# TensorE order of attention pairs 4 to 15: four runs of one array mode a pair, score stages between runs, small pieces evicted together

## The chip, the cores and the metric

The kernel runs on one core of a Trainium2 chip. The metric is the device time of one launch in microseconds (us); the kernel before takes 1127.12 us, the median of 3 runs (1125.73 to 1127.14). TensorE (PE) multiplies matrices and transposes, VectorE (DVE), ScalarE (ACT) and GpSimd (POOL) work on elements, and SyncE (SP) issues most transfers.

## The reference

Attention with a bias from a small network, then two feed-forward layers, all in float32.

```python
# attention: B, H, S, D = 4, 8, 576, 64; hidden 32
scores = q @ k^T / sqrt(D)
x      = log1p(|i - j|) / log1p(max(i, 1))          # (S, S, 1)
bias   = relu(x @ w1 + b1) @ w2                     # (S, S, H), the same for every batch
attn   = softmax(scores + bias);  o = attn @ v
x      = o as (2304 tokens, 512)
# layer 1                                # layer 2
h = x @ w_in;  g = h * cos(h)            # h = x @ w_in;  g = max(h,0) + alpha*min(h,0)
x = g @ w_out                            # out = g @ w_out
```

Sizes of the layers: 512 to 2048 and back, 2304 tokens.

## The kernel before

The attention works on 16 **pairs**: two heads of one batch. The 576 queries of a pair are four tiles of 128 (stages 1 to 4, both heads each) and a remainder of 64, taken for both heads together (stage 0). Tiles 0 and 1 are unit A, tiles 2 and 3 with the remainder unit B. Pairs 0 to 3 run all units A first, since their bias is still being computed; from pair 4 (`FIRST`) on, a pair runs A, then B.

A **score stage** (`emit_S`, L448) is six steps on TensorE. For stages 1 to 4 each step is two matmuls over 64 rows of the array, one head each, side by side; stage 0 uses all 128 rows. All stages write one PSUM tile (`ps_s`, `bufs=1`), so that a stage can start when the two DVE operations of the stage before (L464: add bias, scale, take the minimum of the negated scores) have read it. ACT then takes the exponential in place (L477).

What follows a unit is a list of **fillers** (L585), one letter each: `0` to `3` transpose the probabilities of 128 keys (`T_full`, eight or four 128x128 transposes into one PSUM bank of three, then a copy to SBUF by DVE, "v", or ACT, "a"); `R` does this for the remainder (`T_rem`); `L` and `M` transpose the last 64 keys (`T_last`, and `T_corner` for the remainder); `N` and `O` transpose the reciprocal row sums (`norm`, `norm_last`), copied by ACT; `v w x y z` multiply by V, 128 keys each, the first four with two 64-column halves of the array and `z` with all of it; `x_out` multiplies by the reciprocals and stores.

So TensorE changes between three **modes**: 64 rows (`64*128` in the profile: scores), 128x128 (transposes, stage 0, `z`) and 64 columns (`128*64`: products with V, corners).

**What sets the order.** The program emits a stage, then as many fillers as a credit allows (L693 to L698). Around this a list scheduler with a timing model reorders all engines' instructions, except where `keep_in_program_order` pins them; the matmuls of the attention are not pinned. Beside the attention run conversions of the weights (`conv`, `wi`, `stage_wo`), a few steps after each stage. `stage_wo` makes four high/low pairs per step in one staging buffer (`sw`): ACT copies the high part (L242), POOL subtracts (L244), SP stores (L259), and the next may start when the store has landed. Then the first layer starts (`h_phase0`, L757).

Of the kernel before, what the change touches and what calls it, by code (L numbers as in the profile page):

```python
# [9 lines left out]
F32 = mybir.dt.float32  # L10
# [18 lines left out]
HS = S // 2  # L29
# [41 lines left out]
def attn_mlp_kernel(ctx: ExitStack, tc: tile.TileContext, a: dict, out: bass.AP):  # L71
# [259 lines left out]
    def attention():  # L331
        with ExitStack() as c:
# [47 lines left out]
            def t_bank(name):  # L380
                return turn("t", ps_t).tile([128, 512], F32, tag="t", name=name)
# [52 lines left out]
            def emit_S(n, s):  # L434
                q, k = qk[n][::len(qk[n]) // 2]
                terms = ((q, k),)
                if n >= NFP:
                    qh, ql, kh, kl = qk[n]
                    terms = ((qh, kh), (qh, kl), (ql, kh))
                both = ps_s.tile([128, 4, 512], F32, tag="s", name=f"S{n}_{s}")  # L440
                pss = [both[:, 2 * h:2 * h + 2] for h in range(2 if s else 1)]
                for hf in range(2):
                    for j, (w, m) in enumerate(terms):
                        for h, ps in enumerate(pss):
                            r, i = (slice(64 * h, 64 * h + 64), s - 1) if s else (slice(0, 128), 4)
# [46 lines left out]

            def corner(ps, w):
                for h in range(2):
                    te.matmul(ps[64 * h:64 * h + 64, 256:320], lhsT=w, rhs=ident[:, 64 * h:64 * h + 64],
                              start=True, stop=True)

            def norm_last(n, u):
                Nt[n, u] = t_bank(f"N{n}_{u}")
                corner(Nt[n, u], Rt[n, u][:, 4, :])  # L500

            def norm(n, u):
                t, rem = SIZE[u]
                rb = Rt[n, u]
                ps = Nt.pop((n, u)) if rem else t_bank(f"N{n}_{u}")
                for x in range(t):
                    te.transpose(out=ps[:, 128 * x:128 * x + 128],
                                 in_=rb[:, 2 * x:2 * x + 2, :].rearrange("p a b -> p (a b)"), identity=ident)
                R = x_p.tile([128, 320], F32, tag="R", name=f"R{n}_{u}")
                cpy("a", R[:, 0:QW[u]], ps[:, 0:QW[u]])  # L510
                Rt[n, u] = R

            def cpy(eng, o, i):
                if eng == "a":
                    keep(4, se.activation(out=o, in_=i, func=AF.Copy))
                else:
                    keep(5, ve.tensor_copy(out=o, in_=i))

            def T_full(n, u, k, eng):
                t, rem = SIZE[u]  # L520
                if k == 0:
                    Tt[n, u] = T_p.tile([128, 4, 2, 320], F32, tag="T", name=f"T{n}_{u}")
                ps = t_bank(f"T{n}_{u}_{k}")
                m = 2 // t
                for d in range(m):
                    for h in range(2):
                        for x, i in enumerate(UNIT[u][0]):
                            o = 256 * d + 128 * t * h + 128 * x
                            cc = m * k + d
                            te.transpose(out=ps[:, o:o + 128], in_=Pp[n, i][:, (S + 64) * h + 128 * cc:(S + 64) * h + 128 * cc + 128],  # L530
                                         identity=ident)
                with tc.high_priority(offset=CPRI):
                    cpy(eng, Tt[n, u][:, m * k:m * k + m, :, 0:128 * t], ps.rearrange("p (c h q) -> p c h q", c=m, h=2))

            def T_rem(n, u, eng):
# [7 lines left out]
            def T_corner(n, u):
                T5t[n, u] = t_bank(f"T5{n}_{u}")
                corner(T5t[n, u], Pt[n, 0, 0][:, 512:S])

            def T_last(n, u, eng):
                T5 = T_p.tile([128, 320], F32, tag="T5", name=f"T5{n}_{u}")
                ps = T5t.pop((n, u)) if SIZE[u][1] else t_bank(f"T5{n}_{u}")
                T5t[n, u] = T5  # L550
                for x, i in enumerate(UNIT[u][0]):
                    te.transpose(out=ps[:, 128 * x:128 * x + 128], in_=Pp[n, i][:, 512:640], identity=ident)
                cpy(eng, T5[:, 0:QW[u]], ps[:, 0:QW[u]])

            def PV(n, u, cc):
                v = vt[n]
                w = QW[u]
                if cc == 0:
                    xps[n, u] = turn("x", ps_x).tile([128, 512], F32, tag="x", name=f"x{n}_{u}")
                ps = xps[n, u]  # L560
                if cc == 4:
                    te.matmul(ps[:, 0:w], lhsT=v[:, 512:640], rhs=T5t.pop((n, u))[:, 0:w], start=False, stop=True)
                else:
                    for h in range(2):
                        te.matmul(ps[64 * h:64 * h + 64, 0:w],  # L565
                                  lhsT=v[:, 256 * h + 64 * cc:256 * h + 64 * cc + 64],
                                  rhs=Tt[n, u][:, cc, h, 0:w], start=(cc == 0), stop=False)

            def x_out(n, u):
                hp, b = pairs[n]  # L570
                w = QW[u]
                ps = xps.pop((n, u))
                del Tt[n, u]
# [7 lines left out]
                ve.tensor_tensor(out=x[:, 0:w], in0=ps[:, 0:w], in1=Rt.pop((n, u))[:, 0:w], op=ALU.mult)  # L581
                at0 = b * S + 128 * UNIT[u][0][0]
                sy.dma_start(out=x_d[hp, :, at0:at0 + w], in_=x[:, 0:w])

            def fillers(n, u):  # L585
                t, rem = SIZE[u]
                e = TENG[u]
                ops = {str(k): (0.44, lambda k=k: T_full(n, u, k, e[k])) for k in range(2 * t)}
                ops.update({"vwxyz"[k]: (0.00167 * QW[u], lambda k=k: PV(n, u, k)) for k in range(5)})
                ops["L"] = (0.11 * t, lambda: T_last(n, u, e[4]))  # L590
                ops["N"] = (0.11 * t, lambda: norm(n, u))
                ops["M"] = (0.1, lambda: T_corner(n, u))
                ops["O"] = (0.1, lambda: norm_last(n, u))
# [60 lines left out]
            while i < NS or pend_exp or waiting or fill:  # L654
                new = []
                if i < NS:
                    n, u, s = stages[i]
                    hp, b = pairs[n]
                    more_bias(max(BFIRST + int(BRATE * j), GNEED[s]))
                    for m in range(FIRST, NP):  # L660
# [33 lines left out]
                while fill and (credit > 0 or i >= NS):  # L694
                    d, fn = fill.pop(0)
                    credit -= d
                    fn()
                if not fill:  # L698
                    credit = min(credit, 0.0)
# [491 lines left out]
```

## Time and profile before

| | |
|---|---|
| median of the runs | 1127.12 us |
| profiled execution, its span | 1125.42 us, 1123.6 us |
| PE busy | 1078.8 us (96%) |
| DVE, ACT, POOL busy | 823.8 (73%), 639.7 (57%), 251.3 us (22%) |
| granted TensorE clock | 0.993 of full speed on average |
| chain that ended last | PE 78%, DVE 9%, DMA 6%, ACT 3% |

The attention fills about the first 346 us. A busy share of PE says little here: a matmul's recorded duration covers its way through the array, and the next one starts long before it ends. The time of a step is read from start to start. In the timeline, one row merges equal instructions that follow each other; the first number is the start of the first of them.

### The profile page before, as it was taken

The numbers are of one execution on the slowest core, as the hardware profiler recorded it, in microseconds if no ns is written. First come the engines' busy times: TensorE is split into PE (matmuls) and PEld (weight loads), VectorE is DVE, ScalarE is ACT, GpSimd is POOL, SyncE is SP. The second block draws the span as 40 slices with busy tenths as digits, with TensorE's granted clock in tenths as the row PEclk, the third lists the DMA queues.
The fourth block names the chain that finished last, engine by engine and source line by source line (L and its number), as shares of the span: only waits on it lengthen the run. The fifth ranks groups of instructions, "written<-read, shape, count | busy, mean of one in ns | idle before, by whom it ended". The sixth has DMA issues, their size and how long they took to land.

```text
span 1123.6 us, 18901 instructions
## 1 busy us (share of the span) xinstructions
PE 1078.8 (96%) x7078; PEld 895.2 (80%) x7078; DVE 823.8 (73%) x1336; ACT 639.7 (57%) x1068; POOL 251.3 (22%) x248
## 2 busy tenths in 40 slices
PE   7698999999998998999999999999999999999998
PEld 2245666666666877888799999998888889999998
DVE  8886777777775789787877787857766756767673
ACT  6886767777775555455455454446555534444442
POOL 4304655656433121000000000222322210000000
PEclk9889999999999999999999999999999999999999
DMA  8666645656447774543766445596666649664621
GB/s 276 216 172 194 188 153 184 207 186 232 153 144 276 300 253 150 160 141 124 251 225 201 174 142 196 171 345 210 207 228 205 208 146 344 208 204 127 211 66 48
DMA packets 107659, 219.77 MB, mean 196 GB/s; under 512 B 11568, under 2 KB 57392, under 8 KB 106160
## 3 DMA queue, kind: packets, MB, share of 16 engines
q1 hardware_dynamic: 77104, 157.74, 43.9%
q10 hardware_dynamic: 28032, 50.34, 12.0%
q0 software_dynamic: 2432, 10.49, 2.4%
q8 instruction: 56, 0.92, 0.3%
q14 instruction: 35, 0.29, 0.1%
HBM read 133.98 MB, written 84.56 MB: 194 GB/s over the span
## 4 chain that ended last, share of the span: by engine, by line
PE 78%; DVE 9%; DMA 6%; ACT 3%; issue 2%; POOL 1%; SPq 1%; ACTq 0%; DVEq 0%; POOLq 0%
PE v L1086 17%; PE ob L955 14%; PE h L757 11%; PE oc L955 9%; PE oa L955 8%; PE S L448 6%; PE x_B L565 3%; DVE u L134 3%; PE T_A L530 2%; PE x_A L565 2%; PE T_B L530 2%; DMA a<-g_d 1%; DMA w_d<-sw 1%; DVE P L464 1%; PE bps L139 1%
## 5 line engine op out<-in xcount | busy, mean ns | idle before, releaser
L1086 PE MATMUL v<-x,v 128*128 128x512 f32 (+1 forms) x984 | 198.0, 364 | 0.0
L1086 PEld LDWEIGHTS v<-x,v 128*128 128x128 f32 x984 | 168.5, 189 | 29.5
L757 PE MATMUL h<-xhi,w 128*128 128x512 f32 (+1 forms) x640 | 184.7, 372 | 7.4 <-DVE tb L770 7.0
L757 PEld LDWEIGHTS h<-xhi,w 128*128 128x128 f32 x640 | 116.1, 188 | 30.9 <-issue 7.4
L226 POOL TENSOR_TENSOR wc<-wc,wp 128x512 int32<-128x512 int32 x64 | 85.5, 1337 | 214.2 <-DVE wc L223 162.7
L477 ACT ACTIVATE P<-P,nm 128x576 f32<-128x576 f32 x128 | 98.5, 771 | 42.9 <-DVE nm L464 42.4
L757 PE MATMUL h<-xlo,w 128*128 128x512 f32 (+1 forms) x320 | 118.5, 370 | 0.0
L937 ACT ACTIVATE op<-a 128x768 fp32r<-128x768 f32 x84 | 70.6, 845 | 83.3 <-PE ob L955 27.3
L938 DVE TENSOR_TENSOR op<-a,op 128x768 fp32r<-128x768 f32 x84 | 80.0, 957 | 50.8 <-ACT op L937 49.9
L464 DVE CUSTOM_DVE_ANT_0 P<-S,bt 128x576 f32<-128x576 f32 x128 | 91.9, 753 | 32.0 <-PE S L448 24.4
L937 ACT ACTIVATE op<-b 128x768 fp32r<-128x768 f32 x84 | 70.7, 844 | 67.9 <-PE ob L955 22.2
L938 DVE TENSOR_TENSOR op<-b,op 128x768 fp32r<-128x768 f32 x84 | 79.9, 955 | 32.9 <-ACT op L937 32.8
L955 PE MATMUL ob<-op,wo 128*128 128x384 f32 x432 | 76.4, 336 | 0.0
L1097 DVE SCALAR_TENSOR_TENSOR u<-v,asg,u 128x1024 f32<-128x1024 f32 (+2 forms) x48 | 48.0, 1013 | 38.2 <-ACT u L1096 37.9
L955 PEld LDWEIGHTS ob<-op,wo 128*128 128x128 f32 x432 | 75.1, 188 | 0.0
L765 ACT ACTIVATE ta<-h,quart 128x1024 int32<-128x1024 f32 (+1 forms) x40 | 41.1, 1027 | 52.1 <-PE h L757 25.7
L757 PEld LDWEIGHTS h<-xlo,w 128*128 128x128 f32 x320 | 60.3, 189 | 10.8
L448 PE MATMUL S<-kh,qh 64*128 64x288 f32 (+1 forms) x270 | 53.0, 348 | 13.8 <-DVE nm L464 13.7
L1096 ACT ACTIVATE u<-v,sgn 128x1024 f32<-128x1024 f32 (+2 forms) x48 | 43.0, 898 | 38.7 <-PE v L1086 38.7
L766 DVE SCALAR_TENSOR_TENSOR tb<-ta,h 128x1024 f32<-128x1024 int32 (+1 forms) x40 | 44.4, 1110 | 23.5 <-ACT ta L765 22.5
L134 DVE TENSOR_SCALAR u<-at,thr 128x576 f32<-128x576 f32 (+17 forms) x120 | 54.3, 522 | 2.3 <-PE bps L139 2.2
L217 ACT ACTIVATE wp<-raw 128x512 int32<-128x512 uint32 x64 | 42.5, 664 | 21.6 <-POOL wc L226 10.5
(153 smaller groups left out, 2157.9 us busy)
## 6 DMA issues: line engine op xcount, KB each, us to landing
a<-g_d SPq DMA_DIRECT2D x60, 384.0 KB, 4.9
b<-g_d SPq DMA_DIRECT2D x48, 384.0 KB, 5.3
raw<-in_wi_dram SPq DMA_DIRECT2D x32, 512.0 KB, 4.0
raw<-in_wo_dram SPq DMA_DIRECT2D x32, 512.0 KB, 4.3
g_d<-tb ACTq DMA_DIRECT2D x32, 512.0 KB, 3.1
g_d<-u ACTq DMA_DIRECT2D x28, 512.0 KB, 3.3
bias_d<-be SPq DMA_DIRECT2D x36, 295.5 KB, 3.5
w_d<-sw SPq DMA_DIRECT2D x35, 256.0 KB, 2.6
```

What stands on the lines that cost most here:

```text
L134: ve.tensor_scalar(u[:, 0:n], at[:, 0:n], thr[:, m:m + 1], None, op0=ALU.max)
L226: ge.tensor_tensor(out=c, in0=c, in1=p, op=ALU.add)
L448: te.matmul(ps[:, hf, 0:HS], lhsT=w[r, 128 * i:128 * i + 128], rhs=m[r, c0:c0 + HS], start=(j == 0), stop=(j == len(terms) - 1))
L464: keep(2, ve.tensor_tensor_reduce(out=sn.rearrange("p (a b) -> p a b", a=2), in0=ps[:, :, 0:HS], in1=bt[hp, s].rearrange("p (a b) -> p a b ...
L477: keep(3, se.activation(out=e, in_=e, func=AF.Exp, bias=nm, scale=-1.0, accum_out=sums[n, u][:, col, 0:1]))
L565: te.matmul(ps[64 * h:64 * h + 64, 0:w], lhsT=v[:, 256 * h + 64 * cc:256 * h + 64 * cc + 64], rhs=Tt[n, u][:, cc, h, 0:w], start=(cc == 0) ...
L757: te.matmul(ps, lhsT=w_[:, wx, w], rhs=xx[:, 0:n], start=(j == 0), stop=(j == 11))
L937: se.activation(out=o[:, 0], in_=x, func=AF.Copy)
L938: lows.append(ve.tensor_tensor(out=o[:, 1], in0=x, in1=o[:, 0].bitcast(F32), op=ALU.subtract))
L955: ins = te.matmul(ps[:, m], lhsT=x[:, sl] if L else w[:, sl], rhs=w if L else x, start=first, stop=kk == NK - 1 and n == 2, skip_group_che ...
L1086: ins = te.matmul(both[:, i, 0:a1 - a0], lhsT=w[:, wx, 128 * cc:128 * cc + 128], rhs=x[:, xx, cc, a0 - o:a1 - o], start=(n == 0), stop=(n ...
L1097: ve.scalar_tensor_tensor(out=g, in0=ps, scalar=asg[:, f:f + 1], in1=g, op0=ALU.mult, op1=ALU.max)
```

## The change

From pair 4 on (`steady`) every matmul of the attention is pinned, so that TensorE's order is the order of emission. Stages of a pair come as 1, 0, 2, 3, 4. The fillers carry a kind, and each stage lets out fillers of certain kinds until one of another kind heads the list. That gives four runs a pair: after stage 1 and around stage 0 one of 128x128 work, after stage 2 one of 64-column work, after stage 3 one of 128x128 work, after stage 4 one of 64-column work. What unit A leaves (`L`, `N`, `z`, `x_out`) is a tail that is put into B's first run, and the reverse.

`L` and `N` now share one PSUM bank and are copied together by ACT (128x512), and so are `M` and `O` (128x128). DVE copied `L` before. The tile `R` goes; `T5` holds both.

```diff
-TENG = {"A": "vava-a", "B": "vavava"}
+RUNS = {"A": ("01^23", "vwxy"), "B": ("R0^123", "vwxyMO")}
+TENG = {"A": "vavaaaa", "B": "vavaaaa"}
...
+            first = next(i for i, x in enumerate(stages) if x[0] == FIRST)
+            stages[first:] = [(n, u, s) for n in range(FIRST, NP) for u, s in (("A", 1), ("B", 0), ("A", 2), ("B", 3), ("B", 4))]
+            steady = []
+            tails = []
+            def pe(ins):
+                return tc.keep_in_program_order(ins) if steady else ins
...
+            def pieces(n, u):
+                if (n, u) not in T5t:
+                    T5t[n, u] = T_p.tile([128, 2, 320], F32, tag="T5", name=f"T5{n}_{u}")
+                return T5t[n, u]
+            def T_corner(n, u):
+                Nt[n, u] = t_bank(f"C{n}_{u}")
+                corner(Nt[n, u][:, 0:64], Pt[n, 0, 0][:, 512:S])
+            def norm_last(n, u, eng):
+                ps = Nt.pop((n, u))
+                corner(ps[:, 64:128], Rt[n, u][:, 4, :])
+                cpy(eng, pieces(n, u)[:, :, 256:320], ps[:, 0:128].rearrange("p (a q) -> p a q", a=2))
+            def T_last(n, u):
+                Nt[n, u, 0] = t_bank(f"L{n}_{u}")
+                for x, i in enumerate(UNIT[u][0]):
+                    pe(te.transpose(out=Nt[n, u, 0][:, 128 * x:128 * x + 128], in_=Pp[n, i][:, 512:640], identity=ident))
+            def norm(n, u, eng):
+                ps = Nt.pop((n, u, 0))
...
+                cpy(eng, pieces(n, u)[:, :, 0:256], ps.rearrange("p (a q) -> p a q", a=2))
...
-                return [ops[k] for k in ORDER[u]] + [(0.0, lambda: x_out(n, u))]
+                if steady:
+                    head, rest = RUNS[u][0].split("^")
+                    old = tails.pop() if tails else []
+                    if (n, u) == (NP - 1, "B"):
+                        return old[0:2] + [(*ops[k], 1) for k in head] + old[2:] + [(*ops[k], 1) for k in rest + "MOLN" + "vwxyz"] + [(0.0, out, 1)]
+                    tails.append([(*ops["L"], 1), (*ops["N"], 1), (*ops["z"], 1), (0.0, out, 1)])
+                    return (old[0:2] + [(*ops[k], 1) for k in head] + old[2:] + [(*ops[k], 3) for k in rest] +
+                            [(*ops[k], 2) for k in RUNS[u][1]])
+                return [(*ops[k], 0) for k in ORDER[u]] + [(0.0, out, 0)]
...
+                if steady:
+                    if i >= NS and not pend_exp and not waiting:
+                        fill += tails.pop() if tails else []
+                    want = {1: (0, 1), 0: (0, 3), 2: (0, 2), 3: (0, 1, 3), 4: (0, 2)}[s] if i < NS else range(4)
+                    while fill and fill[0][2] in want:
+                        fill.pop(0)[1]()
```

**TensorE between stage 4 of pair 7 and stage 1 of pair 8.** `S` are the scores (`S_4` stage 4), `x_A` products with V, `N_A` reciprocals, `T_B` and `Tr` transposes. Before:

```order
L448 MATMUL S_4_2625<-kh_2269,ql_2267 128x288 x2
L565 MATMUL x_A<-T_A,v_2110 64x256 x4
L507 MATMUL N_A<-ident,rb_A 128x128 x2
L565 MATMUL x_A<-T_A,v_2110 64x256 x2
L530 MATMUL T_B_2854<-ident,P_2_2579 128x128
L565 MATMUL x_A<-T_A,v_2110 64x256 x2
L562 MATMUL x_A<-T_A,v_2110 128x256
L530 MATMUL T_B_2896<-ident,P_2_2579 128x128
L539 MATMUL Tr_2902<-ident,Pr_2528 128x128 x4
L448 MATMUL S_1_2678<-kh_2518,qh_2515 128x288 x2
```

Now, at the same place:

```order
L457 MATMUL S_4_2665<-kh_2274,ql_2272 128x288 x2
L575 MATMUL x_A<-T_A,v_2140 64x256 x8
L457 MATMUL S_1_2707<-kh_2531,qh_2528 128x288 x2
L457 MATMUL S_1_2707<-kl_2532,qh_2528 128x288 x2
L457 MATMUL S_1_2707<-kh_2531,ql_2529 128x288 x2
L457 MATMUL S_1_2707<-kh_2531,qh_2528 128x288 x2
L457 MATMUL S_1_2707<-kl_2532,qh_2528 128x288 x2
L457 MATMUL S_1_2707<-kh_2531,ql_2529 128x288 x2
L524 MATMUL L_A<-ident,P_0_2446 128x128
L524 MATMUL L_A<-ident,P_1_2547 128x128
L529 MATMUL L_A<-ident,rb_A 128x128 x2
L561 MATMUL Tr_2740<-ident,Pr_2500 128x128 x4
```

Six groups of two modes between the stages have become one group; `N_A` and `Tr` moved behind stage 1.

**TensorE where pair 3 ends and pair 4 begins**, now (`S_3` and `S_4` are pair 3's, `S_1` is pair 4's, `x_B` belongs to pair 2):

```order
L457 MATMUL S_3_1553<-kh_527,ql_525 128x288 x2
L575 MATMUL x_B<-T_B,v_678 64x320 x2
L457 MATMUL S_4_1611<-kh_527,qh_524 128x288 x2
L457 MATMUL S_4_1611<-kl_528,qh_524 128x288 x2
L457 MATMUL S_4_1611<-kh_527,ql_525 128x288 x2
L457 MATMUL S_4_1611<-kh_527,qh_524 128x288 x2
L457 MATMUL S_4_1611<-kl_528,qh_524 128x288 x2
L457 MATMUL S_4_1611<-kh_527,ql_525 128x288 x2
L457 MATMUL S_1_1658<-kh_1508,qh_1505 128x288 x2
```

Before, ten rows of fillers stood between `S_3` and `S_4`, and eight between `S_4` and `S_1`; now two products, and nothing.

**ACT at the end of pair 12**, now (`P_3` is stage 4's probability tile, `P_0` the next pair's; `sw` the staging buffer of `stage_wo`, `wp` and `wc` conversions, `T_A<-L_A` the joint copy):

```order
L243 ACTIVATE sw_3_0_3202<-wc_6_1_3042 128x256
L486 ACTIVATE P_3_3962,sume_118<-P_3_3962,nm_4_3963 128x576
L218 ACTIVATE wp_8_1_3344<-raw_8_1_2977 128x512
L486 ACTIVATE P_3_3962,sume_118<-P_3_3962,nm_8_3965 128x576
L217 ACTIVATE wc_8_1_3343<-raw_8_1_2977 128x512
L243 ACTIVATE sw_3_1_3206<-wt_3_3161 128x2x256
L535 ACTIVATE T_A<-L_A 128x2x256
L486 ACTIVATE P_0_3998,sume_119<-P_0_3998,nm_1_3999 128x576
```

Before, these two staging copies stood in pair 13:

```order
L242 ACTIVATE sw_3_0_3165<-wc_6_1_3014 128x256
L477 ACTIVATE P_0_3944,sume_119<-P_0_3944,nm_5_3947 128x576
L217 ACTIVATE wp_8_1_3354<-raw_8_1_2943 128x512
L216 ACTIVATE wc_8_1_3353<-raw_8_1_2943 128x512
L477 ACTIVATE P_1_3997,sume_119<-P_1_3997,nm_2_3998 128x576
L477 ACTIVATE P_1_3997,sume_119<-P_1_3997,nm_6_4000 128x576
L242 ACTIVATE sw_3_1_3219<-wt_3_3110 128x2x256
L515 ACTIVATE R_B<-N_B 128x320
```

The first staging copy has moved ahead of pair 12's last two exponentials. In either kernel eleven of these copies, ten steps, lead from it to the one just before pair 15's last exponentials (`sw_5_2`).

## Rows read from the trace of the kernel before

**Rows 1.** Stretch, us; busy PE, PEld, DVE, ACT, POOL (instructions); clock, DMA share, GB/s.
```profile
149.43:270.16 120.73, 119.02 (x994) 82.32 (x993) 91.80 (x230) 86.72 (x199) 71.72 (x75) 1.00 0.60 191
270.16:288.00 17.84, 17.84 (x148) 12.15 (x147) 12.90 (x36) 11.91 (x28) 10.14 (x10) 1.00 0.48 176
288.00:307.27 19.27, 17.67 (x147) 12.32 (x147) 14.94 (x38) 13.59 (x30) 8.02 (x8) 1.00 0.50 167
307.27:326.97 19.70, 17.29 (x142) 11.86 (x143) 13.92 (x38) 15.43 (x36) 7.98 (x9) 1.00 0.42 136
```

**Rows 2.** Timeline of PE, end of pair 9: start, us, engine, line, tiles, shape, count.
```profile
230.30 1.47 PE L530 MATMUL T_A<-ident,P 128*128 128x128 f32 x12
231.71 0.40 PE L448 MATMUL S<-kh,qh 64*128 64x288 f32 x2
...
232.69 0.65 PE L565 MATMUL x_A<-T_A,v 128*64 128x256 f32 x4
233.28 0.44 PE L552 MATMUL T_A<-ident,P 128*128 128x128 f32 x2
...
234.60 1.08 PE L565 MATMUL x_A<-T_A,v 128*64 128x256 f32 x8
235.61 0.33 PE L530 MATMUL T_B<-ident,P 128*128 128x128 f32 x1
235.87 0.40 PE L448 MATMUL S<-kh,qh 64*128 64x288 f32 x2
```

**Rows 3.** What PE waited for, 149.43 to 270.16 us, the longest.
```profile
PE S L448 <- DVE nm L464: 0.7, 1, 0.7
```

**Rows 4.** Copies on DVE by form, same stretch: busy us, mean ns.
```profile
L517 DVE COPY T_A<-T_A 128x512 f32<-128x512 f32 x14 | 9.7, 690 | 7.2 <-PE T_A L530 7.2
...
L517 DVE COPY T_B<-T_B 128x320 f32<-128x320 f32 x7 | 3.4, 480 | 0.0
L517 DVE COPY T_A<-T_A 128x256 f32<-128x256 f32 x7 | 2.9, 421 | 0.0
```

**Rows 5.** ACT by form, same stretch.
```profile
L477 ACT ACTIVATE P<-P,nm 128x576 f32<-128x576 f32 x56 | 43.1, 770 | 17.3 <-DVE nm L464 16.8
...
L515 ACT ACTIVATE T_B<-T_B 128x512 f32<-128x512 f32 x14 | 8.3, 590 | 7.1 <-PE T_B L530 7.1
...
L515 ACT ACTIVATE R_B<-N_B 128x320 f32<-128x320 f32 x7 | 3.0, 429 | 0.6 <-PE N_B L507 0.6
```

**Rows 6.** Timeline, all engines: two score stages as close as their tile allows.
```profile
304.58 0.40 PE L448 MATMUL S<-kh,qh 64*128 64x288 f32 x2
...
305.68 0.76 DVE L464 CUSTOM_DVE_ANT_0 P<-S,bt 128x576 f32<-128x576 f32 x1 [0.63 <-PE S L448]
...
306.36 0.75 DVE L464 CUSTOM_DVE_ANT_0 P<-S,bt 128x576 f32<-128x576 f32 x1
...
307.27 0.40 PE L448 MATMUL S<-kh,qh 64*128 64x288 f32 x2 [0.39 <-DVE nm L464]
```

**Rows 7.** Staging copies: a wait (288 to 345 us), SP's first and tenth store issues.
```profile
ACT sw L242 <- DMA w_d<-sw: 5.3, 5, 1.7
...
293.20 0.32 SPq L259 DMA_DIRECT2D w_d<-sw  x1
...
341.21 0.80 SPq L259 DMA_DIRECT2D w_d<-sw  x2
```

**Rows 8.** Stage 4 of pairs 12 and 15, the last product; then windows, of all and L757.
```profile
283.80 0.40 PE L448 MATMUL S<-kh,qh 64*128 64x288 f32 x2
...
342.96 0.40 PE L448 MATMUL S<-kh,qh 64*128 64x288 f32 x2 [0.35 <-DVE nm L464]
...
359.09 0.81 PE L562 MATMUL x_B<-T_B,v 128*128 128x320 f32 x2
...
342.96:359.50 16.54, 13.63 (x89) 9.65 (x89) 8.13 (x19) 8.74 (x20) 6.22 (x6) 1.00 0.85 277
...
342.96:359.50 16.54, 6.00 (x25) 4.38 (x25) 1.00 0.85 277
```

More of the change, by code (lines that the diff above doesn't have):

```diff
@@ L447, in emit_S @@
                             with tc.high_priority(offset=SP if hf + j + h else 0):
-                                te.matmul(ps[:, hf, 0:HS], lhsT=w[r, 128 * i:128 * i + 128], rhs=m[r, c0:c0 + HS],
-                                          start=(j == 0), stop=(j == len(terms) - 1))
+                                pe(te.matmul(ps[:, hf, 0:HS], lhsT=w[r, 128 * i:128 * i + 128], rhs=m[r, c0:c0 + HS],
+                                             start=(j == 0), stop=(j == len(terms) - 1)))
                 if s == 4:
@@ L494, in corner @@
                 for h in range(2):
[L495 to L511, printed above, removed]
+                    pe(te.matmul(ps[64 * h:64 * h + 64], lhsT=w, rhs=ident[:, 64 * h:64 * h + 64],
+                                 start=True, stop=True))
+            def pieces(n, u):
[15 more added lines that the diff above has]
+                ps = Nt.pop((n, u, 0))
+                for x in range(2):
+                    pe(te.transpose(out=ps[:, 256 + 128 * x:384 + 128 * x],
+                                    in_=Rt[n, u][:, 2 * x:2 * x + 2, :].rearrange("p a b -> p (a b)"), identity=ident))
+                cpy(eng, pieces(n, u)[:, :, 0:256], ps.rearrange("p (a q) -> p a q", a=2))
             def cpy(eng, o, i):
@@ L529, in T_full @@
                             cc = m * k + d
-                            te.transpose(out=ps[:, o:o + 128], in_=Pp[n, i][:, (S + 64) * h + 128 * cc:(S + 64) * h + 128 * cc + 128],
-                                         identity=ident)
+                            pe(te.transpose(out=ps[:, o:o + 128], in_=Pp[n, i][:, (S + 64) * h + 128 * cc:(S + 64) * h + 128 * cc + 128],
+                                            identity=ident))
                 with tc.high_priority(offset=CPRI):
@@ L536, in T_rem @@
                 w = 128 * SIZE[u][0]
+                if (n, u) not in Tt:
+                    Tt[n, u] = T_p.tile([128, 4, 2, 320], F32, tag="T", name=f"T{n}_{u}")
                 ps = t_bank(f"Tr{n}")
                 for cc in range(4):
-                    te.transpose(out=ps[:, 128 * cc:128 * cc + 128], in_=Pt[n, 0, 0][:, 128 * cc:128 * cc + 128],
-                                 identity=ident)
+                    pe(te.transpose(out=ps[:, 128 * cc:128 * cc + 128], in_=Pt[n, 0, 0][:, 128 * cc:128 * cc + 128],
+                                    identity=ident))
                 cpy(eng, Tt[n, u][:, :, :, w:w + 64], ps.rearrange("p (c h q) -> p c h q", c=4, h=2))
[L543 to L553, printed above, removed]
             def PV(n, u, cc):
@@ L561, in PV @@
                 if cc == 4:
[L562 removed]
+                    pe(te.matmul(ps[:, 0:w], lhsT=v[:, 512:640], rhs=T5t[n, u][:, 0, 0:w], start=False, stop=True))
                 else:
                     for h in range(2):
[L565 to L567 removed]
+                        pe(te.matmul(ps[64 * h:64 * h + 64, 0:w],
+                                     lhsT=v[:, 256 * h + 64 * cc:256 * h + 64 * cc + 64],
+                                     rhs=Tt[n, u][:, cc, h, 0:w], start=(cc == 0), stop=False))
             def x_out(n, u):
@@ L693, in attention @@
                 credit += PER * (1.85 if s else 1.6)
[L694 to L699, printed above, removed]
+                if steady:
[4 more added lines that the diff above has]
+                        fill.pop(0)[1]()
+                else:
+                    while fill and credit > 0:
+                        d, fn, _ = fill.pop(0)
+                        credit -= d
+                        fn()
+                    if not fill:
+                        credit = min(credit, 0.0)
                 wsteps += SR * m
```

15 lines of the change are left out of this document (9 added, 6 removed).

## The prediction

> **What bounds the kernel now.** I read first the busy times by stretch, then TensorE's waits, then its timeline from start to start, then the last pairs. The first of the rows by stretch is pairs 5 to 11, the others are pairs 12, 13 and 14. Pairs 5 to 11 take 120.73 us, 17.25 each, and in them PE is busy for 119.02 us, while DVE has 13.1 us of work a pair (91.80 / 7) and ACT 12.4 (86.72 / 7) [rows 1]. The longest wait of PE in the whole stretch is 0.7 us [rows 3]. So these pairs are TensorE's, and the question is what a matmul costs there beyond its own steps. The timeline answers it [rows 2]. One transpose between two other modes holds PE for 0.26 us (235.61 to 235.87), two for 0.37 (233.28 to 233.65): a step of 0.11, and 0.15 for coming and going. Products with V do the same: two steps 0.59 (232.69 to 233.28), four 1.01 (234.60 to 235.61), so a step of 0.21 to 0.215 and again 0.15 to 0.16. A score stage holds PE for 0.98 us. Twelve transposes that follow work of their own mode take 1.41, which is 12 steps and 0.10 for leaving. Each visit to a mode thus costs 0.15 us on top, however long it is.
>
> Pairs 13 and 14 are another stage: 19.27 and 19.70 us with PE busy for 17.67 and 17.29 of them [rows 1]. There the staging copies run in a chain through one buffer. The first and the tenth store issue lie 48.0 us apart, 5.3 us a step, and ACT itself stands for 5.3 us in five waits for a store [rows 7].
>
> **The change, part by part.**
>
> *Visits.* The order of the program gives 17 to 20 visits a pair before in pairs 5 to 11, 134 in the seven pairs, 19.1 on average; now eight (four score stages, two 128x128 runs, two 64-column runs). Removed are 11.1 visits of 0.15, which is 1.67 us a pair: 17.25 - 1.67 = 15.58. From the other side, the sum of what is left: four score stages 3.92; stage 0, now inside a run, 0.83 (0.98 less 0.15); 44 transposes of 0.11, 4.84; twenty steps with V, ten of 0.215 and ten of 0.27 (320 columns for 256), 4.85; corners about 0.2; four runs of 0.15, 0.6: 15.24 with no wait at all.
>
> *Waits that the fixed order can meet.* TensorE can no longer be given other work while one operand is late. Three places are tight. A score stage can start 2.69 us after the one before at the earliest, two DVE passes between them [rows 6]; from stage 4 to stage 1 there is now 0.98 + 8 steps + 0.15 = 2.85, a margin of 0.16. Between the end of stage 3 and the passes of stage 4 DVE has two passes of 0.68 (305.68 to 306.36), two copies of 0.69 [rows 4], the product with the reciprocals and in most pairs a conversion. Of DVE's 13.1 us a pair nine passes, four such copies and the two `L` copies leave 3.3 for products, sums and conversions; half of it here makes 4.4. TensorE needs some 3.9 from there (run 2.9, stage 0.98). And `z` comes eight transposes (0.87 us) after the pieces whose joint copy it needs, the copy itself being 0.59 [rows 5]. Walked through with the changed orders of DVE and ACT, each of these is met or missed by 0.1 to 0.3. I take 0.3 a pair: 15.5, between 15.24 and 15.58. Pairs 5 to 11 save 7 x 1.75 = 12.2 us.
>
> *Joint copies.* DVE loses the two `L` copies, 0.42 + 0.48 [rows 4], and has 12.2 us a pair left. ACT copies 512 columns (0.59) instead of 320 (0.43) and of 256, and a new piece of 128 columns; on the line through the two known sizes 256 is 0.38 and 128 is 0.27 [rows 5]. That is 0.64 more, 13.0 a pair. Both stay below 15.5 and cost nothing as a rate.
>
> *Where pair 4 begins.* Stage 3, two products, stage 4 and stage 1 of the next pair stand almost bare. Stage 4 could come 1.7 us after stage 3 begins (0.98, a visit, two steps) and must wait until 2.69, stage 1 could come after 0.98 and must wait likewise [rows 6]: 1.0 + 1.7 = 2.7 lost. Pair 4 has ten visits for twenty (1.5 back), and 1.1 us of its work (the last product of A, six transposes) now lies behind pair 5's first stage. I count 0, between 2.7 lost and 1.5 won.
>
> *Pairs 12 to 15.* The stretch from stage 4 of pair 12 to stage 4 of pair 15 is 342.96 - 283.80 = 59.16 us before [rows 8]. TensorE would now need 3 x 15.5 = 46.5. But ten staging steps lie in it, from the copy ahead of pair 12's last exponentials to the one ahead of pair 15's, and ACT's order ties the exponentials to them. At 5.3 a step that is 53.3 us. So the chain ends later and sets the stretch: 5.9 won. The part of pair 12 before it goes from 13.64 (270.16 to 283.80) to 12.7: 0.9. After stage 4 of pair 15 come the rests, up to 359.50, with 6.0 us of the first layer's matmuls among them and PE idle for 16.54 - 13.63 = 2.9 [rows 8]. Now 2.3 us more work is left there (eight steps and a visit, four transposes), and the first layer's matmuls fill the idle time: 0.5 won.
>
> From there on TensorE's order is the old one, and it starts that much earlier. Sum: 12.2 + 0 + 0.9 + 5.9 + 0.5 = 19.5. Against the profiled execution's 1125.4 us (span 1123.6) that gives 1105.9; the median of the runs, 1127.1, lies 1.7 above it, so I forecast **1107.5 us**. Its own range is 1101 to 1112.
>
> **Rivals.**
>
> *The stores hold the last pairs as before (1115 us).* The staging steps come in uneven places, two of them in one stage and then none; every one that is late now stops a copy or an exponential that TensorE's fixed order needs next. Then the 59.2 us stay, the end loses 1, and 12 us are left of the sum. For it: ACT's waits for stores [rows 7]. Against it: PE was idle for only 1.6 and 2.4 us of pairs 13 and 14 [rows 1]; with 1.7 us less work in each, it would have to be idle for about twice that. The Trainium skill, "PSUM — Partial Sum Buffer", section "Engine vs sequencer instructions", says that ScalarE's queue is strictly first in, first out; by that rule an exponential behind a late staging copy waits although its own operand is there. ACT's idle time before staging copies agrees with it.
>
> *Late joint copies in every pair (1135 us, slower).* If two exponentials (1.54 us) stand before the joint copy, `z` waits 1.54 + 0.59 - 0.87 = 1.26, at A and at B: 2.5 a pair. A pair is then 15.24 + 2.5 = 17.7, seven of them lose 3.4; pairs 13 to 15 take 53.3 + 7.5, 1.6 more than before; the start of pair 4 loses 2.7: about 8 slower. It decides from 2.0 us of wait a pair on (17.25 - 15.24). For it: margins of 0.1 to 0.2 at three places, and no spare work for TensorE. Against it: in ACT's changed order the joint copy of A stands behind stage 4's last exponential, which is done before TensorE reaches the pieces. The Trainium skill, "TensorEngine Tiling (Array Packing)", section "Performance Considerations", warns that a better packed array leaves PSUM evacuation as the bottleneck and asks for both engines; here all small pieces go to one. As a rate the rows don't bear it out (13.0 of 15.5); what is left of that rule is lateness at these places, and it is why this case has more than a twentieth.
>
> *No stalls at all (1097 us).* 15.24 a pair, staging steps below 4.6 us, so that TensorE sets the last pairs (59.16 - 45.7), and pair 4 at its best: 14.1 + 13.4 + 0.9 + 0.5 + 1.5 = 30.4 won. For it speaks only that the scheduler placed DVE's and ACT's work around the new order; against it the margins above, and that the mean step was 5.3.
>
> **How the numbers follow.** Forecast 0.6, stores as before 0.2, late copies 0.11, no stalls 0.05, and 0.04 that waits eat just what the visits give back. What a measurement can tell from no change is about 0.2%, 2.3 us. Faster takes the first, second and fourth case, 0.85; same 0.04; slower 0.11. The range 1098 to 1120 holds the forecast, the stores' case and the milder ends of the others; left out are most of the late copies and half of the stall-free case.
>
> **What would show it.** Right: score stages 1 of pairs 5 to 12 lie 15.2 to 15.9 us apart, with eight mode changes a pair, PE's waits below 0.5 a pair, DVE near 12.2 and ACT near 13.0 busy; pairs 13 to 15 take 17 to 18.5 us with ACT waiting for stores; S_4 to S_1 where pair 4 begins is 2.7. Wrong: PE waits for ACT's joint copies or for DVE's passes of more than 1 us in every pair; a visit that costs more when the run is long; pairs 13 to 15 at 19 or more; or a first layer that starts earlier and then waits for weights, so that the time won is lost again before the layer ends.

## The result, and the profile after

The changed kernel takes 1118.22 us (median of 10 runs, 1116.48 to 1126.11), the kernel before 1127.13 in 10 runs beside it: ratio 0.9912, 95% interval 0.989 to 0.9934. Faster was right, and the time lies inside the range but above the forecast's own (1101 to 1112): of 19.6 us forecast 8.9 came. The profiled execution took 1119.18 us (span 1117.4).

The attention accounts for it; starts of score stages and of the last product, in us:

| stretch | before | after | won | forecast |
|---|---|---|---|---|
| start of pair 5 | 149.43 | 149.63 | -0.2 | 0 |
| pairs 5 to 11 | 120.73 | 115.27 | 5.5 | 12.2 |
| pair 12 up to stage 4 | 13.64 | 14.15 | -0.5 | 0.9 |
| stage 4 of pair 12 to that of 15 | 59.16 | 56.30 | 2.9 | 5.9 |
| from there to the last product | 16.13 | 15.70 | 0.4 | 0.5 |

That is 8.0 us (359.09 to 351.05). The profiled spans differ by 6.2, so 1.8 went again later. The first layer's last product starts at 556.8 us, before at 562.4, which is 5.6 earlier: the loss is in that layer. TensorE's longest wait there was 1.7 us before and is now 3.8 (total, times, longest):

```profile
PE h L785 <- DVE tb L798: 7.6, 4, 3.8
```

Behind that wait, which ends at 544.39, the granted clock is 0.79, 0.50 and 0.86 in the three 2 us windows from 544 on; no window of this layer fell below 0.97 before.

The busy times by stretch, columns as in [rows 1]: pairs 5 to 11, then 12, 13 and 14.

```profile
149.63:264.90 115.27, 110.62 (x994) 86.30 (x994) 86.44 (x218) 90.68 (x208) 72.00 (x75) 0.99 0.65 204
264.90:281.92 17.02, 15.81 (x145) 11.98 (x144) 12.62 (x34) 12.24 (x30) 9.23 (x10) 1.00 0.51 184
281.92:302.35 20.43, 16.12 (x144) 12.20 (x143) 14.62 (x37) 15.20 (x35) 7.70 (x9) 1.00 0.47 154
302.35:320.09 17.74, 15.96 (x142) 12.11 (x142) 13.61 (x34) 13.35 (x31) 6.50 (x7) 1.00 0.48 161
```

DVE has 12.3 us a pair and ACT 13.0, as forecast. New is that PE is not busy for 4.7 us of pairs 5 to 11, where it was 1.7 [rows 1]. A pair is now 16.47 us on average, but the seven are 15.39, 17.13, 16.05, 15.64, 15.76, 19.83 and 15.47: five about as forecast, two not. PE's timeline in one of the five, pair 11, shows the long runs where [rows 2] had short visits:

```profile
255.56 2.37 PE L575 MATMUL x_B<-T_B,v 128*64 128x320 f32 x16
...
258.09 0.40 PE L457 MATMUL S<-kh,qh 64*128 64x288 f32 x2
...
261.07 1.04 PE L550 MATMUL T_A<-ident,P 128*128 128x128 f32 x8
262.04 0.40 PE L457 MATMUL S<-kh,qh 64*128 64x288 f32 x2
...
263.03 1.95 PE L575 MATMUL x_A<-T_A,v 128*64 128x256 f32 x16
264.90 0.40 PE L457 MATMUL S<-kh,qh 64*128 64x288 f32 x2
```

The waits of PE and ACT between 149 and 345 us (total, times, longest; these answer to [rows 3, 7]):

```profile
ACT sw L243 <- DMA w_d<-sw: 8.6, 7, 2.2
...
ACT xhi L768 <- DMA xlo<-x_d: 6.5, 3, 3.4
PE x_A L572 <- ACT T_A L535: 5.9, 4, 2.7
ACT wp L218 <- DMA raw<-in_wo_dram: 4.9, 3, 2.6
...
PE x_B L572 <- ACT T_B L535: 2.3, 1, 2.3
...
PE x_A L572 <- DVE T_B L537: 1.5, 1, 1.5
```

L572 is `z`, and what it waits for is in most cases the joint copy on ACT (L535). The wait of 1.5 us is pair 6's. The profile puts it down to a copy on DVE, but the joint copy, behind an `xhi` for which ACT stood 2.21 us, ended within 0.02 us of it (169.01 and 169.03). With `xhi` on POOL, below, this wait is gone. Before, PE's longest wait in pairs 5 to 11 was 0.7 us. What stands behind the longest is seen in the timeline of all engines in pair 10:

```profile
229.53 0.32 SPq L185 DMA_DIRECT2D xlo<-x_d  x1
...
233.70 0.63 ACT L768 ACTIVATE xhi<-xlo 128x512 fp32r<-128x512 f32 x1 [3.44 <-DMA xlo<-x_d]
234.24 0.58 ACT L535 ACTIVATE T_A<-L_A 128x512 f32<-128x512 f32 x1
...
234.87 1.22 PE L572 MATMUL x_A<-T_A,v 128*128 128x256 f32 x2 [2.74 <-ACT T_A L535]
...
236.13 0.44 PE L457 MATMUL S<-kl,qh 128*128 128x288 f32 x1
236.37 0.44 PE L457 MATMUL S<-kh,ql 128*128 128x288 f32 x1
```

`xhi` splits the first layer's first input tile, work that the first layer needs some 100 us later. Its load was issued at 229.53; ACT stood 3.44 us for it, with the joint copy next in its queue, and `z` stood 2.74. After it the steps of a score stage start 0.24 us apart (236.13 to 236.37) instead of 0.13. The windows of this place (columns as in [rows 1]; the clock is third from last) show why:

```profile
230.00:234.00 4.00, 2.13 (x24) 1.72 (x20) 2.79 (x8) 0.56 (x3) 3.12 (x3) 1.00 0.74 205
234.00:236.00 2.00, 1.13 (x3) 0.95 (x4) 0.00 (x0) 2.00 (x6) 2.00 (x4) 0.63 0.02 6
236.00:238.00 2.00, 2.00 (x11) 1.99 (x10) 0.85 (x2) 0.81 (x3) 2.00 (x2) 0.51 0.20 66
238.00:242.00 4.00, 4.00 (x38) 2.79 (x38) 2.47 (x7) 3.50 (x8) 0.60 (x1) 1.00 0.84 295
```

The granted clock fell to half (1.2 GHz) and came back. Pair 10 is 4.4 us longer than pair 11: 2.7 of wait, and a rest of 1.6, which is about what the slow clock takes ((0.37 + 0.49) x 2 = 1.7 by the two windows).

Pair 13 has the same pattern with the staging copy `sw`, which waits for the store before it:

```profile
291.83 2.36 SPq L260 DMA_DIRECT2D w_d<-sw  x2
...
296.00 0.63 ACT L243 ACTIVATE sw<-wc 128x512 fp32r<-128x512 f32 x1 [1.83 <-DMA w_d<-sw]
296.54 0.58 ACT L535 ACTIVATE T_B<-L_B 128x512 f32<-128x512 f32 x1
...
297.17 0.54 PE L572 MATMUL x_B<-T_B,v 128*128 128x320 f32 x1 [2.29 <-ACT T_B L535]
```

Where pair 4 begins, PE's timeline shows the two forecast waits:

```profile
124.71 0.40 PE L457 MATMUL S<-kh,qh 64*128 64x288 f32 x2 [0.95 <-DVE nm L473]
...
127.40 0.40 PE L457 MATMUL S<-kh,qh 64*128 64x288 f32 x2 [1.63 <-DVE nm L473]
```

and two windows behind them a clock that falls to half:

```profile
128.00:130.00 2.00, 2.00 (x21) 1.30 (x18) 1.49 (x5) 0.80 (x3) 0.41 (x1) 0.68 1.02 342
130.00:132.00 2.00, 2.00 (x10) 1.67 (x11) 1.33 (x4) 1.31 (x3) 2.00 (x3) 0.50 0.97 296
```

The lines that answer to [rows 8], stage 4 of pairs 12 and 15 and the last product:

```profile
279.05 0.40 PE L457 MATMUL S<-kh,qh 64*128 64x288 f32 x2
...
335.35 0.40 PE L457 MATMUL S<-kh,qh 64*128 64x288 f32 x2
...
351.05 0.81 PE L572 MATMUL x_B<-T_B,v 128*128 128x320 f32 x2
```

### The profile page after: what moved, and what is told of

The parts are those of the page before. It is cut to its first block, busy times and chain, and to the rows that moved or that the text cites. A ratio compares the mean times of both kernels' runs of the same rounds, so it can differ in the third digit from the quotient of the medians.

```text
span 1117.4 us, 18861 instructions
## 1 busy us (share of the span) xinstructions
PE 1063.2 (95%) x7078; PEld 900.6 (81%) x7078; DVE 809.9 (72%) x1304; ACT 646.0 (58%) x1084; POOL 255.0 (23%) x248
## 4 chain that ended last, share of the span: by engine, by line
PE 71%; DMA 8%; DVE 6%; ACT 3%; issue 2%; POOL 1%; SPq 0%; ACTq 0%; POOLq 0%; DVEq 0%
PE v L1114 18%; PE ob L983 14%; PE h L785 9%; PE oc L983 9%; PE oa L983 9%; PE S L457 4%; DMA w_d<-sw 3%; PE x_B L575 2%; PE T_B L550 2%; PE T_A L550 1%; DVE tb L794 1%; POOL sw L245 1%; PE x_A L575 1%; DVE tb L795 1%; DVE tb L798 1%
## 5 line engine op out<-in xcount | busy, mean ns | idle before, releaser
L797 ACT ACTIVATE tb<-tb,hpi 128x1024 f32<-128x1024 f32 (+1 forms) x40 | 42.3, 1059 | 24.6 <-DVE tb L795 17.1
L224 DVE SCALAR_TENSOR_TENSOR wc<-raw,wc 128x512 int32<-128x512 int32 x64 | 54.0, 848 | 1.3
```

The source lines that it names most:

```text
L224: ve.scalar_tensor_tensor(out=c, in0=raw[:, :, 1], scalar=-2 ** 31, in1=c, op0=ALU.bitwise_and, op1=ALU.bitwise_xor)
```

## The experiments

Theory 1: ACT's side work that waits for a transfer stands ahead of joint copies, and TensorE's fixed order passes the wait on. Theory 2: ACT has too many copies. Theory 3: the single staging buffer sets pairs 12 to 15. Ratios are to the kernel before, timed on the same chip (the changed kernel's is 0.9912). The scheduler places the other engines anew in each kernel, so no edit moves one wait alone.

**`xhi` on POOL.**

```diff
-                se.activation(out=hi[:, 0:n], in_=r[:, 0:n], func=AF.Copy)
+                if t:
+                    se.activation(out=hi[:, 0:n], in_=r[:, 0:n], func=AF.Copy)
+                else:
+                    ge.tensor_copy(out=hi[:, 0:n], in_=r[:, 0:n])
```

> Only the engine of three copies changes: the high part of the first layer's first input tile (xhi<-xlo) is made by POOL instead of ACT; joint copies stay on ACT. Theory 1 (joint copies stand in ACT's queue behind instructions that wait for a transfer): pair 6 falls from 17.1 to about 15.6 us, pair 10 from 19.8 to about 16, pair 14 from 17.7 to about 16.5, and the waits of PE for T_A after the xlo loads go; pairs 5 to 11 take about 109.9 instead of 115.3 us, the whole kernel is 5 to 6.5 us faster than the changed kernel (about 1112 to 1113). Theory 2 (ACT has too many copies to make): pairs 6 and 10 keep their waits, time within 1 us of the changed kernel (1118).

Measured: 1110.25 us, ratio 0.9821 (0.9789 to 0.9854). Pair 10 fell to 15.68 us, as expected, and no `z` waits in pairs 5 to 11; but pair 6 became 19.79 (15.6 expected), pair 14 18.5 (16.5 expected), and pairs 5 to 11 took 114.3 us (109.9 expected). Pair 6 has another stall, in the timeline of DVE and PE:

```profile
173.57 1.07 DVE L223 TENSOR_SCALAR wc<-wc 128x512 int32<-128x512 int32 x1 [0.18 <-ACT wc L217]
174.68 1.65 DVE L224 SCALAR_TENSOR_TENSOR wc<-raw,wc 128x512 int32<-128x512 int32 x1
...
178.34 0.66 PE L550 MATMUL T_A<-ident,P 128*128 128x128 f32 x4 [1.78 <-DVE T_A L537]
```

and in the window behind it:

```profile
179.00:181.00 2.00, 2.00 (x16) 1.53 (x18) 0.78 (x2) 1.19 (x4) 0.00 (x0) 0.57 0.84 288
```

A conversion on DVE, 2.7 us long here, stood ahead of two passes and a copy; TensorE waited 1.78, and the clock fell again. So theory 1 holds for the waits behind `xhi`, and a second queue can do the same. The time came out below the 1112 to 1113 expected, but only in part where expected: stage 4 of pair 15 starts 6.38 us earlier than in the changed kernel, and of that 1.66 lie ahead of pair 5, 0.95 in pairs 5 to 11, and 3.77 from pair 12 on.

**Joint copies on DVE**, all else as changed.

```diff
-TENG = {"A": "vavaaaa", "B": "vavaaaa"}
+TENG = {"A": "vavavaa", "B": "vavavav"}
```

> The joint copies of L with N and of M with O are made by DVE instead of ACT; all else as changed. Theory 2 (ACT has too many copies to make): all waits of PE for copies go, pairs 5 to 11 at 15.3 to 15.6 us, the kernel 5 to 8 us faster than the changed kernel. Theory 1 (instructions that wait for a transfer hold ACT's queue): z itself no longer waits at pairs 6 and 10, but the transposes' copies and exponentials behind the same ACT instructions still come late, so that only half of the 1.8 and 3.9 us there is won; DVE gets 14 us a pair with the passes of the score stages behind the joint copies, so that S waits more. Between 2 us faster and 3 slower than 1118.

Measured: 1143.28 us, ratio 1.0115 (1.0083 to 1.0146). Pairs 5 to 11 took 138.22 us, and there PE waited for the joint copies in every pair:

```profile
PE x_A L572 <- DVE T_A L537: 10.7, 7, 3.0
PE x_B L572 <- DVE T_B L537: 6.4, 7, 1.7
```

Neither expectation was bad enough. Theory 2 falls: with fewer copies on ACT (85.80 us of 138, instead of 90.68 of 115) the waits are larger. It is the rival of late copies in every pair, on the other engine.

**Four more visits a pair.**

```diff
-RUNS = {"A": ("01^23", "vwxy"), "B": ("R0^123", "vwxyMO")}
+RUNS = {"A": ("01^2", "v3wxy"), "B": ("R0^12", "v3wxyMO")}
...
```

> The last transposes of a unit (filler 3) move from the 128x128 run into the middle of the 64-column run: twelve visits a pair instead of eight, everything else as changed. If a visit costs 0.15 us in place, the seven pairs take 4 x 0.15 x 7 = 4.2 us more (119.5 instead of 115.3) and pairs 4 to 15 about 7 us more: 1125. If what was won came from the smaller number of copies and not from visits: no change, 1118. If the waits of TensorE swallow part of it: 2 to 4 us more.

Measured: 1144.2 us, ratio 1.0119 (1.008 to 1.0157); pairs 5 to 11 took 130.44 us, 15.2 more (4.2 expected). The products now follow their transposes closely, and PE's waits there are 14.1 instead of 5.1 us; 4.2 is left for the visits and 2 unexplained. The price itself is clean in pair 9's unit A, which waits for nothing:

```profile
240.50 0.65 PE L575 MATMUL x_A<-T_A,v 128*64 128x256 f32 x4
241.08 0.66 PE L550 MATMUL T_A<-ident,P 128*128 128x128 f32 x4
241.67 1.52 PE L575 MATMUL x_A<-T_A,v 128*64 128x256 f32 x12
243.12 0.40 PE L457 MATMUL S<-kh,qh 64*128 64x288 f32 x2
```

This run is 2.62 us, the one of transposes before stage 4 is 0.53 (238.98 to 239.51); in the changed kernel's pair 11 they are 1.87 and 0.97. So two visits cost 0.31, 0.155 each.

**Runs emitted, but nothing pinned.**

```diff
-                return tc.keep_in_program_order(ins) if steady else ins
+                return ins
```

> The program emits the four runs as changed, but the matmuls are not pinned, so that the scheduler sets TensorE's order: 17 to 20 visits a pair again, joint copies kept. By the visits' price pairs 5 to 11 take about 7 x 1.6 = 11 us more than without stalls, that is 109 + 11 = 120 us, and the kernel about 1124 to 1128, as before the change; TensorE then waits for no joint copy (below 1 us in all). If the visits cost nothing and the joint copies were the gain: about 110 us and 1112.

Measured: 1146.97 us, ratio 1.0132 (1.0086 to 1.0179), slower than expected. Pairs 5 to 11 have 18.6 visits each and take 137.48 us: 22.2 more, of which the visits make 7 x 10.6 x 0.15 = 11.1 and PE's waits (11.5 instead of 5.1) 6.4; the rest, 4.7, is open. Without the pins this order of emission is worse than the old one.

**`xhi` and `sw` on POOL.** Beside the first edit, in `split_to`:

```diff
-        se.activation(out=hi, in_=w, func=AF.Copy)
+        if pinned:
+            se.activation(out=hi, in_=w, func=AF.Copy)
+        else:
+            ge.tensor_copy(out=hi, in_=w)
```

> As the kernel with xhi<-xlo on POOL, and the high parts of stage_wo (sw<-wc, sw<-wt) are made by POOL too, so that no instruction of ACT waits for a store any more. Theory 1 (ACT instructions that wait for a transfer hold joint copies): TensorE's waits for ACT's copies in pairs 12 to 15 (3.7 us with only xhi moved) go to below 1, pairs 13 and 14 take 17 to 17.5 us instead of 18.8 and 18.5, and from stage 4 of pair 12 to that of pair 15 it is 51 to 52 instead of 54.1 us: 2 us faster than with xhi alone. Theory 3 (the single staging buffer's chain of copy, subtraction and store sets these pairs): a step is not shorter, POOL waits for the stores in place of ACT, and the splits of the next pair's q and k stand behind it: 54 us or more, no gain.

Measured: 1107.41 us, ratio 0.98 (0.9767 to 0.9832), the lowest of all, though its interval overlaps that of `xhi` alone. From stage 4 of pair 12 to that of pair 15 it is 51.98 us. All of PE's waits there, and POOL's longest between 258 and 323 us:

```profile
PE S L460 <- DVE nm L476: 2.1, 4, 0.7
PE T_A L553 <- DVE T_A L540: 1.3, 1, 1.3
PE T_B L553 <- DVE T_B L540: 0.2, 1, 0.2
...
POOL sw L246 <- DMA w_d<-sw: 20.1, 6, 4.5
```

No `z` waits. POOL stands 20.1 us for the stores, and none of TensorE's waits there is for POOL. The chain itself is slower: eleven staging copies span 66.9 us (269.98 to 336.88), in the changed kernel 56.9 (280.32 to 337.25), so that eight of them fall into the stretch instead of ten. A slower chain and a shorter stretch: the chain doesn't set it, and theory 1 has it against theory 3. Pair 13 took 17.57 us, near the 17 to 17.5 expected, pair 14 18.67.

**Two staging buffers.**

```diff
-            t = wpool["t"].tile([128, 2, 2, 256], F32R, tag="st", name=f"st{f}").rearrange("p a b c -> p a (b c)")
+            t = wpool["t"].tile([128, 2, 2, 256], F32R, tag="st", bufs=STB[bool(pinned)], name=f"st{f}").rearrange("p a b c -> p a (b c)")
...
```

(`STB = (2, 1)`; the same in `leave_w`. For room, the attention's output tile goes from two buffers to one, and a temporary of the first layer from three to two.)

> Two staging buffers instead of one, all copies on ACT as changed. For room, the attention's output tile has one buffer instead of two, and a temporary of the first layer two instead of three, so that only the attention is compared. Theory 3 (the chain through the single buffer sets the last pairs): ACT's waits for stores (8.6 us in the changed kernel) fall below 2, the staging steps come closer together, and from stage 4 of pair 12 to that of pair 15 it is 49 to 51 instead of 56.3 us. Theory 1 alone: the stalls at z of pairs 13 and 15 go (2.3 us each), the others (xhi in pair 14, wp in pair 12) stay: 52 to 53. If neither: 55 to 57.

Measured: 1132.65 us, ratio 1.0006 (0.9984 to 1.0028); the stretch takes 57.27 us. There ACT's waits for stores fell from 6.6 to 2.4 us, and `z` waits as before:

```profile
PE x_A L573 <- ACT T_A L536: 3.2, 3, 1.6
ACT sw L244 <- DMA w_d<-sw: 2.4, 2, 1.4
PE x_B L573 <- ACT T_B L536: 2.2, 2, 1.1
```

Theory 3 expected 49 to 51 us: without most of the stores' waits the stretch is no shorter. Loads (`wp`, 2.9) and other instructions now stand ahead of the joint copies. The run is not a clean one, though: fourteen staging copies instead of ten fall into the stretch, so that ACT is busy for 47.42 us of it instead of 43.33, and what the single output buffer costs was not tested apart.

**More fillers before pair 4**, with `xhi` on POOL.

```diff
+                if first - 3 <= i < first:
+                    credit += 1.0
```

> xhi<-xlo on POOL, and the last three score stages before pair 4 let out one microsecond more of fillers each, so that stages 3 and 4 of pair 3 and stage 1 of pair 4 no longer stand bare; the rest of the order is the same. In the changed kernel TensorE stood for 2.7 us there and had half its clock for some 3 us right after. If both are the price of the bare place: stage 1 of pair 5 comes 2.5 to 4 us earlier against the start of pair 3's last stages, no clock below 1 between 120 and 140 us, the kernel 2.5 to 4 us faster than with xhi alone. If my account of the prediction held (nothing lost at this place): no change within 1 us.

Measured: 1116.56 us, ratio 0.988 (0.985 to 0.991). From stage 3 of pair 3 to stage 1 of pair 5 it is 25.54 us; with `xhi` alone 27.51, in the changed kernel 27.62. No clock below 0.97 there. So the fillers are worth 2 us against these two kernels, which have a spell of slow clock there. They are worth less elsewhere: the same stretch is 26.27 us with `xhi` and `sw` on POOL, and 26.18 in the next run, which has the same two waits and no window under 0.97. But the last pairs took 60.0 us, with one `z` waiting 3.1 us for ACT, and the clock fell behind it: a small edit 180 us earlier had moved the side work.

**One group of staging steps fewer**, with `xhi` on POOL.

```diff
-NIP, H0R, H1R = 3, 1.9, 7.0
+NIP, H0R, H1R = 4, 1.9, 7.0
```

> xhi<-xlo on POOL, and one of the five groups of staging steps (four copies, subtractions and stores) is left to the first layer, where three groups already are: sixteen steps in the attention instead of twenty. Theory 3: the chain ends about four steps (20 us) earlier, so that the last one or two pairs are TensorE's: from stage 4 of pair 12 to that of pair 15 it is 47 to 50 instead of 54.1 us, and the attention ends 4 to 6 us earlier; if the first layer takes up the steps for nothing, the kernel is that much faster (about 1106), otherwise 1108 to 1111. Theory 1 alone: two waits at z fewer, 52 us.

Measured: 1115.03 us, ratio 0.9872 (0.984 to 0.9904), slower than expected; the stretch from stage 4 of pair 12 to that of pair 15 took 54.68 us. It again held ten staging copies, so this run tells little on theory 3.

**Joint copy undone, first try.**

```diff
+                cpy("v", pieces(n, u)[:, 0, 0:256], Nt[n, u, 0][:, 0:256])
...
-                cpy(eng, pieces(n, u)[:, :, 0:256], ps.rearrange("p (a q) -> p a q", a=2))
+                cpy(eng, pieces(n, u)[:, 1, 0:256], ps[:, 256:512])
```

> The order as changed, but the joint copy of L and N is undone: DVE copies L (128x256) right after its transposes, ACT copies N (128x256), as before the change; xhi, sw and the rest on ACT as changed. It prices the joint copies apart from the order. Theory 1: z needs only L's piece, so it no longer stands behind ACT's waits for transfers at pairs 6, 10, 13 and 14 (7 us with the slow clock), but L's copy stands in DVE's queue behind passes and conversions instead, as the joint copies did when all were on DVE (2.0 us of wait a unit there); the copies of the transposes, still on ACT, stay late. Between 4 us faster and 6 slower than the changed kernel. If the joint copies are a gain by their number (theory 2 reversed): slower by 12 x 0.4 = 5 us. If only the engine's order of work counts, and DVE's is free here: 5 to 7 us faster.

Measured: 1179.27 us, ratio 1.0418 (1.0375 to 1.0461), a miss by my edit: the first copy stands in `T_last`, before N's transposes into the same tile, and PE (pinned) waits for it, in all between 140 and 420 us:

```profile
PE L_A L530 <- DVE T_A L538: 21.4, 9, 5.2
PE L_B L530 <- DVE T_B L538: 20.0, 13, 2.9
```

**Both gains together**: `xhi` and `sw` on POOL, and the credit.

> xhi<-xlo and the high parts of stage_wo on POOL, and one microsecond more of fillers after each of the last three stages before pair 4. If the two gains add up: stage 1 of pair 5 comes 26.3 - 25.5 = 0.8 to 2 us earlier after stage 3 of pair 3, pairs 12 to 15 as with POOL alone (52.0 us from stage 4 of pair 12 to that of pair 15), no wait at z: about 1105.5. If the scheduler's other choices move with the credit, as in the run with the credit and sw on ACT (60.0 instead of 54.1 us in the last pairs), the last pairs are 54 or more and the gain is lost: 1107 to 1110.

Measured: 1109.03 us, ratio 0.9807 (0.9767 to 0.9847): no better than without the credit. Stage 3 of pair 3 to stage 1 of pair 5 is 25.51 us (0.8 less), the last pairs are 53.1 (1.1 more).

**Joint copy undone, both copies behind the transposes.**

```diff
-                cpy(eng, pieces(n, u)[:, :, 0:256], ps.rearrange("p (a q) -> p a q", a=2))
+                cpy("v", pieces(n, u)[:, 0, 0:256], ps[:, 0:256])
+                cpy(eng, pieces(n, u)[:, 1, 0:256], ps[:, 256:512])
```

> As the last one, without its fault: there the copy of L stood between L's and N's transposes, which share a PSUM tile, so that TensorE itself waited for it (21.4 + 20.0 us). Now both are transposed first; then DVE copies L (128x256) and ACT copies N (128x256). The order and all else as changed. Theory 1 (a joint copy that stands in ACT's queue behind a wait for a transfer makes z late): z needs DVE's copy alone, its waits for ACT at pairs 6, 10, 13, 14 go, and new ones for DVE come, whose queue holds passes and conversions: 1112 to 1124. If the joint copies by themselves are a gain of some size: 1124 or more, with ACT and DVE no busier by rate than 13.2 of 16 us a pair. If DVE is simply the better engine: 1111.

Measured: 1144.17 us, ratio 1.013 (1.0094 to 1.0166), far above the 1112 to 1124 of theory 1. `z` waits for DVE's copy of L, between 140 and 360 us:

```profile
PE x_A L573 <- DVE T_A L538: 14.8, 11, 2.7
PE x_B L573 <- DVE T_B L538: 9.0, 12, 1.5
```

**Joint copies alone**: the lines that set `steady` and the new order of stages are taken out.

> The joint copies alone: the order of stages, fillers and TensorE's instructions is left as before the change (17 visits a pair, the scheduler free), but L and N, M and O share a bank and are copied together by ACT. By the prediction's account (joint copies cost and bring nothing as a rate; the gain is the visits'): the time of the kernel before, 1127 to 1131, pairs 5 to 11 at 120 to 122 us. If the joint copies carry the gain: about 1118. If joint copies on ACT are late wherever they stand: over 1135, with TensorE waiting for them.

Measured: 1129.28 us, ratio 0.9998 (0.9972 to 1.0025); the first layer's last product starts at 563.5 us, before at 562.4. Inside the attention the free order shifted (stage 1 of pair 5 comes 5.2 us earlier, stage 4 of pair 15 4.1 later, with one spell of slow clock), so that its 129.74 us for pairs 5 to 11 can't be set against the 120 to 122 expected. In the time of the whole, the joint copies by themselves change nothing that can be measured.

## Why the prediction was right, and where it was not

The direction and the mechanism of the gain held, and its size came to less than half of the forecast. That the time lies in the range is owed to the range's upper part, which was there for the rival with the stores.

**Visits: right.** Eight a pair, 0.15 us each (0.155 by the extra visits), and pairs without a long wait at 15.4 to 16.1. The gain is the order's: joint copies alone give nothing. From the kernel before, the sum for pairs 5 to 11 is 120.73 less 11.7 for the visits, plus 3.6 for PE's longer waits (5.1 us instead of 1.5) and about 1.6 of slow clock: 114.2, and 115.27 were measured.

**"I take 0.3 a pair" for waits: the step that failed.** The pairs came 1.2 us each above the sum without waits (16.47 against 15.24), 8.6 in the seven: 5.1 are PE's waits and about 1.6 the slow clock. Of the 6.7 us lacking against the forecast, 6.0 are in pairs 6 and 10. The step named `z` as tight and looked for exponentials ahead of the joint copy. It did not ask which of ACT's instructions wait for a transfer, though ACT's waits before the change (149 to 345 us) held them:

```profile
ACT xhi L740 <- DMA xlo<-x_d: 2.5, 2, 1.3
```

They were shorter then, and the free order had other work for TensorE meanwhile: no wait of PE in pairs 5 to 11 was over 0.7 [rows 3]. Taking `xhi` off ACT put pair 10 at 15.68. The Trainium skill, "PSUM — Partial Sum Buffer", section "Engine vs sequencer instructions", has the rule (ScalarE's queue is strictly first in, first out); the trace agrees, with a copy whose last transposes start at 230.87 and which itself starts at 234.24, right behind `xhi`. I had used that rule for the stores alone.

**Slow clock: not counted at all.** It added about 1.6 us to the 2.7 of the worst wait, and by the two windows an estimated 1.6 where pair 4 begins (0.32 x 2 + 0.50 x 2). There the two stages stand 2.70 and 2.69 us apart, as forecast. That the forecast of 0 held to 0.2 is luck in part: from stage 3 of pair 3 to stage 1 of pair 5 it is 27.62 us instead of 26.08, and stage 3 comes 1.3 us earlier.

**Joint copies: right as a rate, with a dependence missed.** They cost nothing, but the fixed order needs them on ACT: with `L` on DVE, as before, it is slower than no change. The rival of late copies in every pair is thus real for DVE, whose passes and conversions stand ahead. The Trainium skill, "TensorEngine Tiling (Array Packing)", section "Performance Considerations", asks for both engines in evacuation; here 1143 us on DVE against 1118 on ACT says that for these copies the queue ahead of them matters more than the split of the load.

**Pairs 12 to 15, "the chain ends later and sets the stretch": wrong.** 56.3 us instead of 53.3. The ten steps took 56.9 us (5.7 each, 5.3 in the sum), but it is not the chain that sets the pairs: on POOL the same ten steps took 66.9, and the stretch fell to 52.0. What counts is what stands behind the waiting instruction. The rival with the stores had that mechanism, though not loads among its causes; its 12 us of gain is the nearest to the 8.9 measured.

Open: why TensorE waits longer for DVE in the first layer, where the 1.8 us went, and why the unpinned order is 15 us worse than the old one.

## What to carry to other kernels

When an engine's order is pinned, list for every engine that feeds it which instructions wait for a transfer, and what stands behind them: here they cost TensorE little while the scheduler could fill them, and up to 2.7 us at a time after. Move such side work to an engine whose queue feeds nothing urgent; here two kinds of copies on POOL more than doubled the gain (ratio 0.9912 to 0.98). What the same move would give without the pinned order was not tested. Fewer mode changes paid, but the waits that remain are longer, and some of them cost clock as well.

## What the hardware showed beyond that

From 120 to 370 us no 2 us window of the kernel before has a granted clock under 0.97. The changed kernel has two spells at half clock there, about 3 us each, the joint copies on DVE five. One followed a wait of 2.74 us, one a wait of 1.78 (pair 6 with `xhi` on POOL); after the wait of 2.29 at 297.17 it did not fall. Where pair 4 begins, waits of 0.95 and 1.63 us were followed by such a spell in the changed kernel; in the run with one group of staging steps fewer the same two, 0.94 and 1.63, were not. So the length of a wait alone does not tell here whether the clock falls.
